# Two experts with split products: the moving parts side by side, 448 + 224 columns in place of 3 x 224

## The chip, the cores and the metric

The kernel runs on one core of a Trainium2 chip, as one program. TensorE (PE) multiplies and transposes, VectorE (DVE) and ScalarE (ACT) work on tiles in SBUF and PSUM, GpSimd (POOL) moves and combines, SyncE (SP) issues most of the DMAs. The metric is the device time of one execution in microseconds (us), the median of several runs.

## The reference

Attention, then a mixture of experts, then a gated MLP over the same 1792 rows:

```python
scores = where(mask, -1e9, q @ k.T / sqrt(64))          # 4 x 12 heads, 448 x 64, causal
x = softmax(scores) @ v                                 # -> (1792, 768)
# experts: the 14336 pairs (token, expert) in descending order of x @ w_gate;
# each token goes to one expert, each of the 8 experts takes 224 tokens
h = np.maximum(x[mask] @ w1[e], 0.0)                    # 224 x 768 @ 768 x 1024
out[mask] = h @ w2[e]                                   # 224 x 1024 @ 1024 x 768
gate = 1.0 / (1.0 + np.exp(-(x @ w_gate)))              # 768 -> 1536
val = x @ w_val
return (gate * val) @ w_out                             # 1536 -> 768
```

Inputs and outputs are fp32 (the weights of the MLP come as 64-bit numbers that the kernel converts).

## The kernel before

**Stages.** Attention until about 285 us; routing and the eight experts until 603.6; the MLP for the first 896 rows (`moe2a`) until about 878; for the other 896 rows (`moe2b`, with seven products of half size in place of eight) until the end. Line 778 (`mm`) issues nearly all matmuls.

**Two kinds of products.** Experts 0 to 5 multiply in fp32. Experts 6 and 7 (`SPLIT`, line 670) and the MLP use split numbers: each operand is a high part, rounded to the matmul's fast 32-bit format, and a low part, the rest. A product then takes three passes: high weight by high token part, high by low, low by high (`prod`, lines 835 to 843; `prods`, line 781, in the MLP).

**An expert.** `xprep` (line 810) transposes the 224 gathered rows into `xx`, 6 blocks of 128 features by 224 tokens; for experts 6 and 7 ACT writes the high part to `xx` (line 823), DVE the low part to `xl` (line 825). `moe` (line 830) runs two layers. Layer 1: 8 outputs of 128 features, each the sum of 6 products; two outputs share one PSUM tile `g` of 512 columns. ACT takes relu and the high part (line 862), DVE the low part (line 864), both 448 wide, into `hx`. Layer 2: 6 outputs, each the sum of 8 products over `hx`. For experts 6 and 7 ACT copies an output to `x2f` (line 895), and after expert 7 the tile is stored to DRAM (line 897) for `moe2b`. The weights of experts 6 and 7 come as `raw`; ACT line 689 writes the high part, DVE line 690 the low part, into two of eight rotating buffers `w`, which PE frees as it goes.

**The start of the MLP.** `conv_split` (lines 79 to 95) makes high and low parts of the MLP weights: lines 83, 85 and 93 on ACT, 87, 88, 89, 92 and 94 on DVE, from a buffer `cs` (two of them) that lines 74 and 77 load; the converted weights are stored to `wsc` by lines 719 (from `ca`), 724 and 725 (high and low part of an output chunk). A gate product goes through a sigmoid on ACT (line 964), is multiplied with the value product on DVE (line 967) and split into `hx` (`h_parts`: ACT line 944, DVE line 945). The tile of the sigmoid lies in memory that the experts' tiles held, `x2f` among them, so the first sigmoid waits for the store of line 897. After two such blocks `out_stage` (line 906) multiplies `hx` with the output weights, in 84 passes of 384 columns.

**What sets the order.** PE's instructions stand in the order of the code. A scheduler places those of the other engines, once, before the program runs; on the chip each engine works through its own list in order, and an instruction that waits holds all behind it. PSUM tiles `g` rotate among 7 buffers.

Of the kernel before, what the change touches and what calls it, by code (L numbers as in the profile page):

```python
# [7 lines left out]
F32 = mybir.dt.float32  # L8
F32R = mybir.dt.float32r
# [3 lines left out]
AF = mybir.ActivationFunctionType  # L13
OP = mybir.AluOpType
# [6 lines left out]
CAP = 224  # L21
E = 8
KD = 6
# [7 lines left out]
def body(ctx: ExitStack, tc: tile.TileContext, q, k, v, moe_w_gate, moe_w1, moe_w2,  # L31
         w_gate2, w_val2, w_out2, out):
    nc = tc.nc
# [171 lines left out]
    ms = att.enter_context(tc.manual_schedule())  # L205
# [261 lines left out]
    mp = ctx.enter_context(tc.tile_pool(name="mp", bufs=2))  # L467
    ps = ctx.enter_context(tc.tile_pool(name="ps", bufs=1, space=PSUM))
# [303 lines left out]
    def use(key):  # L772
        while key not in W:
            load_chunk()
        return W[key]

    def mm(o, a, b, first, last_):
        nc.tensor.matmul(o, a, b, start=first, stop=last_)  # L778
        tick(max(b.shape[-1] * (4.0 if b.dtype == F32 else 1.0) / 2.4, 107.0))
# [9 lines left out]
    XE, X2, X2F = {}, {}, {}  # L789
# [3 lines left out]
    def gathers():  # L793
        while gat["n"] <= gat["x"] and gat["n"] in have:
            with tc.high_priority(HO):
                gather(gat["n"])
            gat["n"] += 1
# [12 lines left out]
    def xprep(ph):  # L810
        xs = XE[ph]
        sp = ph in SPLIT
        xx = mo.tile([128, KD, CAP], F32R if sp else F32, name="xx", bufs=2)
        xl = mo.tile([128, KD, CAP], F32R, name="xl", bufs=1) if sp else None
        for dp in range(3):
            w = ps.tile([128, 512], F32, name="g", bufs=7)[:, :4 * P].rearrange("p (a h q) -> p a h q", a=2, h=2)
            for h in range(2):
                for dd in range(2):
                    d = 2 * dp + dd
                    nc.tensor.transpose(w[:, dd, h, :], xs[h][:, d * 128:(d + 1) * 128], ident[:P, :P])  # L820
            wf = w.rearrange("p a h q -> p a (h q)")
            dd_ = slice(2 * dp, 2 * dp + 2)
            nc.scalar.activation(xx[:, dd_], wf, AF.Copy)
            if sp:
                nc.vector.tensor_tensor(xl[:, dd_], wf, xx[:, dd_].bitcast(F32), op=OP.subtract)
        XE[ph] = (xx, xl) if sp else xx
        gat["x"] = ph + 1
        gathers()

    def moe(ph, nxt):  # L830
        xx = XE[ph]
        hs_ = []
        sp = ph in SPLIT

        def prod(o, w, x, first, last_):

            if sp:
                (wh_, wl_), (xh_, xl_) = w, x
                mm(o, wh_, xh_, first, False)
                mm(o, wh_, xl_, False, False)  # L840
                mm(o, wl_, xh_, False, last_)
            else:
                mm(o, w, x, first, last_)

        def each(t, f):
            return tuple(f(x) for x in t) if sp else f(t)
        for c in range(4):
            w = each(use(("w1", ph, c)), lambda t: t.rearrange("p (c f) -> p c f", c=KD))
            if c % 2 == 0:
                if sp:  # L850
                    h2 = mp.tile([128, 2, 4, CAP], F32R, name="hx", bufs=3)
                    hs_.append((h2[:, 0], h2[:, 1]))
                else:
                    hs_.append(mp.tile([128, 4, CAP], F32, name="hx", bufs=3))
            g = ps.tile([128, 512], F32, name="g", bufs=7)
            for f in range(2):
                for d in range(KD):
                    prod(g[:, f * CAP:(f + 1) * CAP], each(w, lambda t: t[:, d, f * 128:(f + 1) * 128]),
                         each(xx, lambda t: t[:, d]), d == 0, d == KD - 1)
            hx = each(hs_[c // 2], lambda t: t[:, 2 * (c % 2):2 * (c % 2) + 2])  # L860
            gg = g[:, :2 * CAP].rearrange("p (a t) -> p a t", a=2)
            nc.scalar.activation(hx[0] if sp else hx, gg, AF.Relu)
            if sp:
                nc.vector.scalar_tensor_tensor(hx[1], gg, 0.0, hx[0].bitcast(F32), op0=OP.max, op1=OP.subtract)
        blk, half = divmod(ph, 2)
        if half == 0:
            if blk < 2:
                X2[blk] = [[xq() for _ in range(2)] for _ in range(2)]
            else:
                X2F[blk] = mo.tile([128, KD, 448], F32, name="x2f", bufs=2)  # L870
        xo = slice(half * CAP, (half + 1) * CAP)
        ws = [use(("w2", ph, c)) for c in range(2)]
        for dp in range(0, KD, 2):
            ys = [ps.tile([128, 512], F32, name="g", bufs=7) for _ in range(2 if dp == 0 else 1)]
            yo = [ys[0][:, :CAP], ys[1][:, :CAP] if dp == 0 else ys[0][:, CAP:2 * CAP]]
            if dp == 2:
                ws += [use(("w2", ph, c)) for c in range(2, 4)]
            for f0, f1 in ((0, 6), (6, 8)) if dp == 0 else ((0, 8),):
                for n in range(2):
                    d = dp + n  # L880
                    for f in range(f0, f1):
                        a = each(ws[2 * (d // 3) + f // 4], lambda t: t.rearrange("p (c f) -> p c f", c=4)
                                 [:, f % 4, (d % 3) * 128:(d % 3) * 128 + 128])
                        prod(yo[n], a, each(hs_[f // 4], lambda t: t[:, f % 4]), f == 0, f == 7)
                    if nxt is not None and f1 == 8 and d == 4:
                        route_until(nxt)
                        with tc.high_priority(HO):
                            xprep(nxt)
            for n in range(2):
                if blk < 2:  # L890
                    x2h, x2l = (t[(dp + n) // 3][:, (dp + n) % 3, xo] for t in X2[blk])
                    nc.scalar.activation(x2h, yo[n], AF.Copy)
                    nc.vector.tensor_tensor(x2l, yo[n], x2h.bitcast(F32), op=OP.subtract)
                else:
                    nc.scalar.activation(X2F[blk][:, dp + n, xo], yo[n], AF.Copy)
        if blk >= 2 and half:
            nc.sync.dma_start(x2_d[blk - 2], X2F[blk])

    def xq():
        return mp.tile([128, 3, 448], F32R, name="xq", bufs=8)  # L900
# [149 lines left out]
    with tc.tile_pool(name="mo", bufs=2) as mo:  # L1050
        route_until(0)
        for _ in range(3):
            step()
        with tc.high_priority(HO):
            xprep(0)
        for ph in range(E):
            moe(ph, ph + 1 if ph + 1 < E else None)
# [32 lines left out]
```

## Time and profile before

| | |
|---|---|
| median of 3 runs | 1127.73 us (1127.5 to 1129.85) |
| profiled execution | 1128.0 us, span 1126.2 us, mean granted clock 0.981 |
| PE busy | 1077.0 us (96%) |
| DVE busy | 696.0 us (62%) |
| ACT busy | 439.6 us (39%) |
| POOL busy | 276.1 us (25%) |
| chain that ended last | PE 77%, DVE 9%, DMA 8%, other 6% |

A matmul's duration in the trace runs from its start to the modelled end of its results; it overlaps the next one. How fast PE goes is read from start to start. PEld is the load of the weights, which each matmul has. [...]

### The profile page before, as it was taken

To read this page: it belongs to the slowest core of one execution; us is meant where nothing else is said; L and a number is where in the kernel's file an instruction comes from. 1 tells how busy PE (TensorE), PEld (TensorE's weight loads), DVE (VectorE), ACT (ScalarE), POOL (GpSimd) and SP (SyncE) were. 2 spreads that over 40 slices of the span, in tenths; PEclk is the share of its full clock that TensorE was granted. 3 is DMA by queue.
4 is the path that set the end of the run, shared out by engine and by line. 5 is a ranking of instruction groups with operands and counts; after the bars stand their busy time and mean duration, and the time that the engine had idled before them with its cause. 6 is when DMAs were issued, how large, how long until landed. Compare 5 with 4: busy or idle time off the path is not lost.

```text
span 1126.2 us, 19875 instructions
## 1 busy us (share of the span) xinstructions
PE 1077.0 (96%) x7401; PEld 1021.0 (91%) x7401; DVE 696.0 (62%) x1980; ACT 439.6 (39%) x846; POOL 276.1 (25%) x379
## 2 busy tenths in 40 slices
PE   6999999982999999999999999999999999999997
PEld 6999999971899999999999899889999999999997
DVE  5777777766545565451566889787745526445545
ACT  4767777740110110122454664433424343323320
POOL 7333333300000000000000000500034846546522
PEclk9999999995899999999999999999999999999999
DMA  9556565525687657777654785654421521230212
GB/s 167 125 123 169 116 165 124 145 77 103 212 218 177 141 181 173 177 190 209 214 169 162 253 268 208 238 202 151 152 84 53 187 96 45 90 107 29 85 56 98
DMA packets 156991, 167.26 MB, mean 149 GB/s; under 512 B 74576, under 2 KB 140128, under 8 KB 156640
## 3 DMA queue, kind: packets, MB, share of 16 engines
q1 hardware_dynamic: 153472, 154.74, 46.3%
q0 software_dynamic: 2496, 11.04, 5.2%
q8 instruction: 58, 0.95, 0.4%
q10 hardware_dynamic: 928, 0.23, 0.1%
q14 instruction: 37, 0.30, 0.1%
HBM read 122.32 MB, written 32.64 MB: 138 GB/s over the span
## 4 chain that ended last, share of the span: by engine, by line
PE 77%; DVE 9%; DMA 8%; issue 2%; ACT 2%; POOL 2%; POOLq 0%; DVEq 0%; ACTq 0%; SPq 0%
PE g L778 54%; PE o L348 8%; PE w L328 4%; DMA wsc<-ca 3%; PE s L295 2%; PE s L296 2%; DMA xg<-x_d,ids 2%; PE w L257 1%; DVE ca L89 1%; DVE ca L92 1%; DVE ca L88 1%; PE r L503 1%; DMA cs<-in_moe_w_out_dram 1%; DVE acc L934 1%; PE g L820 1%
## 5 line engine op out<-in xcount | busy, mean ns | idle before, releaser
L778 PE MATMUL g<-xq,w 128*128 128x448 f32 x1188 | 281.6, 367 | 0.0
L778 PEld LDWEIGHTS g<-xq,w 128*128 128x128 f32 x1188 | 222.7, 188 | 20.8
L778 PE MATMUL g<-w,hx 128*128 128x384 f32 x1008 | 182.3, 338 | 4.4 <-DVE hx L945 2.3
L778 PEld LDWEIGHTS g<-w,hx 128*128 128x128 f32 x1008 | 176.0, 189 | 9.5 <-DVE hx L945 5.8
L778 PE MATMUL g<-xx,w 128*128 128x224 f32 x768 | 151.5, 339 | 0.0
L778 PE MATMUL g<-hx,w 128*128 128x224 f32 x864 | 150.8, 331 | 0.0
L778 PEld LDWEIGHTS g<-hx,w 128*128 128x128 f32 x864 | 137.6, 191 | 1.7
L778 PEld LDWEIGHTS g<-xx,w 128*128 128x128 f32 x768 | 135.1, 191 | 2.1
L778 PE MATMUL g<-xs,w 128*128 128x448 f32 x432 | 124.7, 365 | 0.0
L742 POOL TENSOR_TENSOR w<-cs,w 128x384 fp32r<-128x384 f32 x84 | 84.2, 1022 | 114.1 <-ACT w L741 113.6
L348 PE MATMUL o<-vt,pt 112*112 112x65 f32 x960 | 106.3, 258 | 0.0
L348 PEld LDWEIGHTS o<-vt,pt 112*112 112x112 f32 x960 | 102.0, 178 | 0.0
L298 DVE CUSTOM_DVE_ANT_0 sm<-s,mask 112x112 f32<-112x112 f32 (+1 forms) x192 | 78.5, 444 | 23.2 <-PE s L296 23.0
L306 ACT ACTIVATE sm<-sm,mn 112x112 f32<-112x112 f32 (+1 forms) x192 | 90.4, 522 | 5.2 <-DVE mn L298 5.1
L934 DVE TENSOR_TENSOR acc<-g,acc 128x384 f32<-128x384 f32 x140 | 74.7, 551 | 28.7 <-PE g L778 28.6
L803 POOL DMA_INDIRECT xg<-x_d,ids x16 | 15.4, 961 | 297.3 <-DVE ids L622 106.7
L778 PEld LDWEIGHTS g<-xs,w 128*128 128x128 f32 x432 | 81.1, 188 | 6.2
L268 POOL CAST st<-hi 64x448 fp32r<-64x448 f32 x96 | 53.3, 556 | 133.7 <-ACT hi L263 115.5
L741 ACT ACTIVATE w<-cs 128x384 fp32r<-128x384 f32 x84 | 40.1, 518 | 95.2 <-PE g L778 59.7
L295 PE MATMUL s<-st,st 128*112 128x112 f32 (+1 forms) x192 | 62.3, 340 | 2.9 <-POOL st L268 2.7
L328 PE MATMUL w<-ident,sm 112*112 112x112 f32 x480 | 63.1, 262 | 0.1
L296 PE MATMUL s<-lo,qz 128*112 128x112 f32 (+1 forms) x192 | 56.7, 310 | 0.0
(214 smaller groups left out, 1448.2 us busy)
## 6 DMA issues: line engine op xcount, KB each, us to landing
w<-in_moe_w_dram SPq DMA_DIRECT2D x96, 384.0 KB, 5.8
raw<-in_moe_w_dram SPq DMA_DIRECT2D x32, 384.0 KB, 4.4
cs<-in_moe_w_gate_dram SPq DMA_DIRECT2D x12, 768.0 KB, 4.3
cs<-in_moe_w_val_dram SPq DMA_DIRECT2D x12, 768.0 KB, 4.7
wsc<-ca SPq DMA_DIRECT2D x24, 384.0 KB, 4.6
cs<-in_moe_w_out_dram SPq DMA_DIRECT2D x12, 768.0 KB, 5.0
wsc<-w SPq DMA_DIRECT2D x12, 768.0 KB, 3.7
cs<-wsc SPq DMA_DIRECT2D x24, 384.0 KB, 3.6
```

The lines of the kernel that those rows point to most:

```text
L268: nc.gpsimd.tensor_copy(st[r, h], hi[r].bitcast(F32))
L295: nc.tensor.matmul(ss[j], qq[:, j, qs], kh[:, j, :w], start=True, stop=False)
L296: nc.tensor.matmul(ss[j], QZ[u % NZ][:, j, qs], kl[:, :w], start=False, stop=True)
L298: nc.vector.tensor_tensor_reduce(sm[:, j, :w], ss[j], mask[:, S - w:], op0=OP.add, op1=OP.min, scale=1.0, scalar=3.0e38, accum_out=mn[:, j ...
L306: nc.scalar.activation(sm[:, j, :w], sm[:, j, :w], AF.Exp, bias=mn[:, j:j + 1], scale=-1.0)
L328: nc.tensor.transpose(w[:P, n, :], sm[:, j, c * P:(c + 1) * P], ident[:P, :P])
L348: nc.tensor.matmul(o[:, n, j, :], pt[:, j * (i + 1) + c, :], vt[:, j, c, :], start=c == 0, stop=c == i)
L741: nc.scalar.activation(hi, src, AF.Copy)
L742: nc.gpsimd.tensor_tensor(lo, src, hi.bitcast(F32), op=OP.subtract)
L778: nc.tensor.matmul(o, a, b, start=first, stop=last_)
L803: g_ = nc.gpsimd.indirect_dma_start(out=xg, out_offset=None, in_=x_d[:], in_offset=bass.IndirectOffsetOnAxis(ap=ids[ph][:, h:h + 1], axis=0))
L934: nc.vector.tensor_tensor(ac, po[:, :384], ac, op=OP.add)
```

## The change

For experts 6 and 7 the high and the low part of the tokens lie side by side: `x2` is 6 blocks of 2 x 224, and `hx` 4 x (2 x 224). A product is one pass of the high weights over all 448 columns and one pass of the low weights over the 224 high columns, into the left half of the same output. So an output has two halves, left (high by high, low by high) and right (high by low), which are summed: ACT copies the right half to a new tile `sd` (two buffers), DVE adds it to the left half. In layer 1 the sum goes back to PSUM, and relu (ACT) and low part (DVE) follow, 224 wide per output; in layer 2 the sum goes to `x2f`. In the last product of an output the two passes stand in the other order. Each output now has a PSUM tile of its own. `xx` of experts 0 to 5 has one buffer in place of two.

```diff
     def xprep(ph):
...
-        xx = mo.tile([128, KD, CAP], F32R if sp else F32, name="xx", bufs=2)
-        xl = mo.tile([128, KD, CAP], F32R, name="xl", bufs=1) if sp else None
+        xx = mo.tile([128, KD, CAP], F32, name="xx", bufs=1) if not sp else None
+        x2 = mo.tile([128, KD, 2, CAP], F32R, name="x2", bufs=1) if sp else None
...
-            nc.scalar.activation(xx[:, dd_], wf, AF.Copy)
             if sp:
-                nc.vector.tensor_tensor(xl[:, dd_], wf, xx[:, dd_].bitcast(F32), op=OP.subtract)
+                nc.scalar.activation(x2[:, dd_, 0], wf, AF.Copy)
+                nc.vector.tensor_tensor(x2[:, dd_, 1], wf, x2[:, dd_, 0].bitcast(F32), op=OP.subtract)
+            else:
+                nc.scalar.activation(xx[:, dd_], wf, AF.Copy)
...
             if sp:
-                (wh_, wl_), (xh_, xl_) = w, x
-                mm(o, wh_, xh_, first, False)
-                mm(o, wh_, xl_, False, False)
-                mm(o, wl_, xh_, False, last_)
+                (wh_, wl_), xf = w, x.rearrange("p b t -> p (b t)")
+                ms = [(o, wh_, xf), (o[:, :CAP], wl_, xf[:, :CAP])]
+                for n_, (o_, a, b) in enumerate(ms[::-1] if last_ else ms):
+                    mm(o_, a, b, first and n_ == 0, last_ and n_ == 1)
...
+                o = g[:, :2 * CAP] if sp else g[:, f * CAP:(f + 1) * CAP]
+                for d in range(KD):
+                    prod(o, each(w, lambda t: t[:, d, f * 128:(f + 1) * 128]), xx[:, d], d == 0, d == KD - 1)
                 if sp:
...
+                    h2 = hx[:, 2 * (c % 2) + f]
+                    tmp = mo.tile([128, CAP], F32, name="sd", bufs=2)
+                    nc.scalar.activation(tmp, o[:, CAP:], AF.Copy)
+                    nc.vector.tensor_tensor(o[:, :CAP], o[:, :CAP], tmp, op=OP.add)
+                    nc.scalar.activation(h2[:, 0], o[:, :CAP], AF.Relu)
+                    nc.vector.scalar_tensor_tensor(h2[:, 1], o[:, :CAP], 0.0, h2[:, 0].bitcast(F32), op0=OP.max,
+                                                   op1=OP.subtract)
...
-            ys = [ps.tile([128, 512], F32, name="g", bufs=7) for _ in range(2 if dp == 0 else 1)]
+            ys = [ps.tile([128, 512], F32, name="g", bufs=7) for _ in range(2 if dp == 0 or sp else 1)]
...
+                elif sp:
+                    tmp = mo.tile([128, CAP], F32, name="sd", bufs=2)
+                    nc.scalar.activation(tmp, yo[n][:, CAP:], AF.Copy)
+                    nc.vector.tensor_tensor(X2F[blk][:, dp + n, xo], yo[n][:, :CAP], tmp, op=OP.add)
```

What the scheduler makes of it, at three places (before expert 6 every engine's list is as it was). Lines behind `moe` carry numbers higher by 14 to 16 in the changed kernel: 980 is the sigmoid (964 before), 960 and 961 are `h_parts` (944, 945), 948 the copy to `acc` (932), 913 the store of `x2f` (897).

First place: PE in expert 7, from the last products of layer 1 (`g_7903`, `g_7864`) to the first of layer 2; `w_7893` and `w_7942`, after the change `w_7836` and `w_7882`, are high parts of weights, `w_7894`, `w_7943`, `w_7837` and `w_7883` low parts. Before:

```order
L778 MATMUL g_7903<-xx_7686,w_7893 128x224
L778 MATMUL g_7903<-xl_7687,w_7893 128x224
L778 MATMUL g_7903<-xx_7686,w_7894 128x224
L778 MATMUL g_7962<-hx_7754,w_7942 128x224 x2
L778 MATMUL g_7962<-hx_7754,w_7943 128x224
```

After:

```order
L778 MATMUL g_7864<-x2_7643,w_7836 128x448
L778 MATMUL g_7864<-x2_7643,w_7837 128x224 x2
L778 MATMUL g_7864<-x2_7643,w_7836 128x448
L778 MATMUL g_7902<-hx_7706,w_7882 128x448
L778 MATMUL g_7902<-hx_7706,w_7883 128x224
```

The two passes with high weights became one of 448 columns; long and short passes alternate, but for the turned last product of an output.

Second place: ACT in expert 7, from the last conversions of w2 (line 689) on; `hx_7853` and `hx_7799` are the second half of the hidden features. Before:

```order
L689 ACTIVATE w_8025<-raw_8027 128x768
L689 ACTIVATE w_8025<-raw_8031 128x768
L862 ACTIVATE hx_7853<-g_7903 128x448
L895 ACTIVATE x2f_7517<-g_7962 128x224
L895 ACTIVATE x2f_7517<-g_7963 128x224
L93 ACTIVATE w_8143<-ca_8150 128x768
L93 ACTIVATE w_8143<-ca_8163 128x768
L895 ACTIVATE x2f_7517<-g_8014 128x224 x2
L93 ACTIVATE w_8258<-ca_8265 128x768
L85 ACTIVATE sq_8276<-cs_8273 128x768
L895 ACTIVATE x2f_7517<-g_8085 128x224 x2
```

After:

```order
L689 ACTIVATE w_7954<-raw_7960 128x768
L866 ACTIVATE sd_7877<-g_7864 128x224
L868 ACTIVATE hx_7799<-g_7846 128x224
L868 ACTIVATE hx_7799<-g_7864 128x224
L908 ACTIVATE sd_7936<-g_7902 128x224
L908 ACTIVATE sd_7939<-g_7903 128x224
L93 ACTIVATE w_8049<-ca_8056 128x768
L93 ACTIVATE w_8049<-ca_8069 128x768
L908 ACTIVATE sd_7996<-g_7942 128x224
L908 ACTIVATE sd_7999<-g_7943 128x224
L908 ACTIVATE sd_8036<-g_8002 128x224
L908 ACTIVATE sd_8039<-g_8003 128x224
```

One relu of 448 became a copy and two relus of 224 behind the same conversions; the last two copies of an output moved ahead of the third line 93 and of line 85. On DVE the matching adds and the subtract stand behind the two conversions of line 690 in the same way, and the four adds of the later outputs among lines 87 to 92.

Third place: SP around the second load of a gate chunk. Before:

```order
L74 DMA cs_8528<-in_moe2_w_val_dram 128x6x256
L724 DMA wsc_63<-w_8373 128x1536
L725 DMA wsc_63<-w_8374 128x1536
L74 DMA cs_8630<-in_moe2_w_gate_dram 128x6x256
L719 DMA wsc_63<-ca_8520 128x768
```

After:

```order
L74 DMA cs_8434<-in_moe2_w_val_dram 128x6x256
L724 DMA wsc_63<-w_8279 128x1536
L74 DMA cs_8536<-in_moe2_w_gate_dram 128x6x256
L725 DMA wsc_63<-w_8280 128x1536
L719 DMA wsc_63<-ca_8426 128x768
```

The load went ahead of the second store; it feeds the line 83 that stands ahead of a copy of `hx` on ACT. That piece of ACT's list, `hx_8286` and `hx_8192` being the second of the two blocks that the first output stage reads. Before:

```order
L83 ACTIVATE cs_8630<-cs_8630 128x768
L93 ACTIVATE w_8513<-ca_8533 128x768
L85 ACTIVATE sq_8633<-cs_8630 128x768
L944 ACTIVATE hx_8286<-g_8308 128x448
L964 ACTIVATE gv_8349<-g_8330 128x448
```

After:

```order
L83 ACTIVATE cs_8536<-cs_8536 128x768
L960 ACTIVATE hx_8192<-g_8214 128x448
L93 ACTIVATE w_8419<-ca_8439 128x768
L85 ACTIVATE sq_8539<-cs_8536 128x768
L980 ACTIVATE gv_8255<-g_8236 128x448
```

The copy of `hx` moved ahead of lines 93 and 85.

## Rows read from the trace of the kernel before

**Rows 1.** Busy table by stage: busy us by engine (instructions), clock, DMA share, GB/s.

```profile
285.00:603.60 318.60, 317.46 (x2456) 308.35 (x2457) 165.81 (x663) 74.39 (x142) 13.04 (x14) 1.00 0.68 183
603.60:878.60 275.00, 270.85 (x1379) 252.37 (x1378) 209.96 (x287) 125.86 (x184) 46.22 (x35) 0.99 0.53 181
```

**Rows 2.** The same table (PE, PEld, DVE, ACT, POOL), 5 us of expert 7.

```profile
575.00:580.00 5.00, 5.00 (x47) 5.00 (x47) 2.36 (x3) 2.45 (x4) 0.00 (x0) 1.00 0.90 292
```

**Rows 3.** Time line of PE: start us, length us, instructions merged, their count.

```profile
554.21 13.56 PE L778 MATMUL g<-hx,w 128*128 128x224 f32 x120
...
571.46 0.27 PE L778 MATMUL g<-xx,w 128*128 128x224 f32 x1
...
603.62 29.36 PE L778 MATMUL g<-xq,w 128*128 128x448 f32 x144
...
651.17 29.92 PE L778 MATMUL g<-xq,w 128*128 128x448 f32 x144
```

**Rows 4.** Time line of matmuls and weight loads (PEld): expert 6; before 632.81.

```profile
553.89 0.19 PEld L778 LDWEIGHTS g<-xl,w 128*128 128x128 f32 x1
553.99 0.27 PE L778 MATMUL g<-xl,w 128*128 128x224 f32 x1
554.00 0.19 PEld L778 LDWEIGHTS g<-xx,w 128*128 128x128 f32 x1
...
632.61 0.56 PEld L778 LDWEIGHTS g<-w,hx 128*128 128x128 f32 x3
```

**Rows 5.** Groups by line and shape: count, busy us, mean ns, idle before.

```profile
L893 DVE TENSOR_TENSOR xq<-g,xq 128x224 fp32r<-128x224 f32 x24 | 9.2, 383 | 5.2 <-ACT xq L892 5.1
...
L895 ACT ACTIVATE x2f<-g 128x224 f32<-128x224 f32 x20 | 6.3, 352 | 18.6 <-PE g L778 18.6
```

**Rows 6.** Time line of DVE and ACT where layer 1 of expert 7 ends.

```profile
588.50 1.83 DVE L690 TENSOR_TENSOR w<-raw,w 128x768 fp32r<-128x768 f32 x2 [1.66 <-ACT w L689]
590.25 0.62 DVE L864 SCALAR_TENSOR_TENSOR hx<-g,hx 128x448 fp32r<-128x448 f32 x1
...
587.62 1.58 ACT L689 ACTIVATE w<-raw 128x768 fp32r<-128x768 f32 x2 [2.01 <-PE g L778]
589.11 0.53 ACT L862 ACTIVATE hx<-g 128x448 fp32r<-128x448 f32 x1
```

**Rows 7.** Chain that ended last, 586 to 640: start us, length us, what.

```profile
594.33 0.85 ACT w L93
...
604.56 9.79 DMA x_d<-x2f
...
623.74 7.96 DMA cs<-in_moe_w_gate_dram
...
631.72 0.90 ACT cs L83
...
635.22 0.51 DVE hx L945
```

**Rows 8.** Time line of PE: first output stage of the MLP, later one.

```profile
632.81 0.69 PE L778 MATMUL g<-w,hx 128*128 128x384 f32 x3
634.64 0.62 PE L778 MATMUL g<-w,hx 128*128 128x384 f32 x2 [1.14 <-ACT hx L944]
635.81 15.53 PE L778 MATMUL g<-w,hx 128*128 128x384 f32 x79 [0.55 <-DVE hx L945]
...
818.04 14.73 PE L778 MATMUL g<-w,hx 128*128 128x384 f32 x84
832.61 27.64 PE L778 MATMUL g<-xq,w 128*128 128x448 f32 x133
```

**Rows 9.** Busy table as in rows 1, single microseconds, clock last but two.

```profile
636.00:637.00 1.00, 1.00 (x4) 1.00 (x4) 1.00 (x2) 0.00 (x0) 0.00 (x0) 0.54 0.00 0
...
638.00:639.00 1.00, 1.00 (x5) 1.00 (x4) 1.00 (x2) 1.00 (x2) 0.00 (x0) 0.50 0.73 209
```

**Rows 10.** Time line of SP's queue: the second store of w.

```profile
622.83 0.34 SPq L725 DMA_DIRECT2D wsc<-w  x1
```

More of the change, by code (lines that the diff above doesn't have):

```diff
@@ L822, in xprep @@
             dd_ = slice(2 * dp, 2 * dp + 2)
-            nc.scalar.activation(xx[:, dd_], wf, AF.Copy)
             if sp:
-                nc.vector.tensor_tensor(xl[:, dd_], wf, xx[:, dd_].bitcast(F32), op=OP.subtract)
-        XE[ph] = (xx, xl) if sp else xx
+                nc.scalar.activation(x2[:, dd_, 0], wf, AF.Copy)
+                nc.vector.tensor_tensor(x2[:, dd_, 1], wf, x2[:, dd_, 0].bitcast(F32), op=OP.subtract)
+            else:
+                nc.scalar.activation(xx[:, dd_], wf, AF.Copy)
+        XE[ph] = x2 if sp else xx
         gat["x"] = ph + 1
@@ L845, in each @@
         def each(t, f):
-            return tuple(f(x) for x in t) if sp else f(t)
+            return tuple(f(x) for x in t) if isinstance(t, tuple) else f(t)
         for c in range(4):
@@ L849, in moe @@
             if c % 2 == 0:
-                if sp:
[L851 to L864, printed above, removed]
+                hs_.append(mp.tile([128, 4, 2, CAP], F32R, name="hx", bufs=3) if sp
+                           else mp.tile([128, 4, CAP], F32, name="hx", bufs=3))
+            hx = hs_[c // 2]
+            gs_ = []
+            for f in range(2):
+                if sp or f == 0:
+                    g = ps.tile([128, 512], F32, name="g", bufs=7)
+                o = g[:, :2 * CAP] if sp else g[:, f * CAP:(f + 1) * CAP]
+                for d in range(KD):
+                    prod(o, each(w, lambda t: t[:, d, f * 128:(f + 1) * 128]), xx[:, d], d == 0, d == KD - 1)
+                if sp:
+                    h2 = hx[:, 2 * (c % 2) + f]
[5 more added lines that the diff above has]
+                                                   op1=OP.subtract)
+            if not sp:
+                nc.scalar.activation(hx[:, 2 * (c % 2):2 * (c % 2) + 2],
+                                     g[:, :2 * CAP].rearrange("p (a t) -> p a t", a=2), AF.Relu)
         blk, half = divmod(ph, 2)
@@ L873, in moe @@
         for dp in range(0, KD, 2):
-            ys = [ps.tile([128, 512], F32, name="g", bufs=7) for _ in range(2 if dp == 0 else 1)]
-            yo = [ys[0][:, :CAP], ys[1][:, :CAP] if dp == 0 else ys[0][:, CAP:2 * CAP]]
+            ys = [ps.tile([128, 512], F32, name="g", bufs=7) for _ in range(2 if dp == 0 or sp else 1)]
+            if sp:
+                yo = [y[:, :2 * CAP] for y in ys]
+            else:
+                yo = [ys[0][:, :CAP], ys[1][:, :CAP] if dp == 0 else ys[0][:, CAP:2 * CAP]]
             if dp == 2:
@@ L883, in moe @@
                                  [:, f % 4, (d % 3) * 128:(d % 3) * 128 + 128])
-                        prod(yo[n], a, each(hs_[f // 4], lambda t: t[:, f % 4]), f == 0, f == 7)
+                        prod(yo[n], a, hs_[f // 4][:, f % 4], f == 0, f == 7)
                     if nxt is not None and f1 == 8 and d == 4:
```

## The prediction

> **What bounds the kernel now.** I read the busy table by stage first. From 285 to 603.6 us (routing and the eight experts) PE is busy 317.5 of 318.6 us, from 603.6 to 878.6 (first half of the gated MLP) 270.9 of 275 [rows 1]. In the two experts that the change touches, DVE and ACT are each busy about 2.4 us of 5 and PE 5.0 of 5 [rows 2]. So PE sets the pace there, and what counts is the distance from the start of one pass to the start of the next, not the mean of a matmul (which overlaps its neighbours).
>
> The time line of PE gives those distances. 120 passes of 224 columns take 13.56 us, the last one's own 0.27 included: 119 starts in 13.29, 111.7 ns each. 144 passes of 448 columns from 603.62 on take 29.36 with 0.37 for the last: 202.7 ns each; 144 from 651.17 on need 206.6 [rows 3]. Twice the columns cost 1.8 times, not twice. The reason shows in the loads: each weight load starts about 10 ns after the matmul before its own, and its own matmul starts about 100 ns later [rows 4]. One load is ahead and no more; before a 448-column pass the load starts 0.20 us ahead, that is again with the pass before [rows 4]. A 224-column pass is therefore as long as the load that runs under it.
>
> Then I followed the chain that ended last through the end of expert 7. It leaves PE at 594.3 and comes back to PE's work only through hx: the conversion of the first MLP weights, the store of x2f (9.8 us from 604.56), the load of a gate weight (8.0 us from 623.74), ACT line 83 at 631.72 and the low part of hx at 635.2 [rows 7]. PE waits for it in the first output stage of the MLP: 84 passes take from 632.81 to 651.17, 18.36 us, where the same 84 later take 14.57 (818.04 to 832.61) [rows 3, 8]. [...]
>
> **The change part by part.** *Passes.* 192 products (2 experts, 2 layers, 48 each) have three passes of 224 now: 576 x 111.7 = 64.3 us. Afterwards each has one of 448 and one of 224. A 448-column pass hides the load of its follower; the 224-column pass that follows has the next load under it and stays at 111.7. Pair: 202.7 + 111.7 = 314.4 ns, 192 of them 60.4 us, so -4.0 us; with 206.6 it is -3.2. No row shows the two lengths in turn. I take -3.6, midway, since both rows are the same shape and neither is nearer.
>
> [...]
>
> *Summing and copying.* Per output the change adds an ACT copy of the right half, a DVE add, and splits the old 448-wide relu and subtract in two. Nearest rows: 224 wide, ACT 352 ns, DVE 383 ns [rows 5]. In the first layer of an expert: ACT 16 x 0.352 less 4 x 0.53 = +3.5 us, DVE 16 x 0.383 less 4 x 0.62 = +3.6 [rows 5, 6]; in the second: DVE 6 x 0.383 = +2.3, ACT nothing (six copies before, six now). About 6 us of DVE and 3.5 of ACT in some 30 us in which each is half idle [rows 2]: hidden by PE as long as PE is never the one that waits.
>
> It waits where layer 1 turns into layer 2. The last two conversions of w2 can start only when PE has freed the buffer, and stand ahead of the last relu on ACT and of the last subtract on DVE, before and after (second place of the order). Now: ACT 587.62, DVE till 590.33, hx whole at 590.87 [rows 6]; layer 2 starts at 571.46 + 144 x 0.1117 = 587.54 and needs it 36 passes, 4.02 us, on, at 591.56. Spare: 0.7 us. Afterwards in expert 7: add behind the two conversions (2.71 after 587.62), then 0.38 + 0.35 + 0.38 and three hand-overs of 0.05: 3.97; needed 13 products x 0.314 = 4.09 after the start of layer 2, which is 4.01 on the same count. Spare: nothing. In expert 6 a subtract stands between the two conversions on DVE, so 0.3 late. I put down +0.35 us for both turns; bounds 0 and +1.5.
>
> *Buffers.* Outputs take 8 and 6 PSUM tiles per expert in place of 4 and 4, out of 7 that rotate; seven outputs ahead is 7 x 1.9 = 13 us of PE, against chains of 2 to 4 us: nothing. One copy of xx in place of two: its readers are done a whole layer before the next is written: nothing. The transposed input goes to the same three copies and subtracts.
>
> *What follows.* So PE enters the MLP 3.25 us earlier, near 600.4. Does the chain behind it come earlier too? The conversions of the first MLP weights wait for w buffers that PE frees (594.3 now) and move with PE by some 2.8 us. On DVE four adds of 0.38 stand among them, 1.5 us if none falls into a gap, so the chain moves by 1.3 to 2.8; I take 2. The store of x2f gains more: now the last two copies stand behind ACT lines 93 and 85, which wait for DVE; in the new order all four copies stand ahead of them. Last product 600.4, copy and add 0.35 + 0.38 and hand-overs: store issued near 601.2 in place of 604.56, landing near 610.6 to 611, and the sigmoid that waits for it 3.5 us earlier.
>
> And one transfer changes its place: the second gate load stood behind both stores of w, the later issued at 622.83, and took 8.0 us [rows 7, 10]; it now goes between them (third place), which takes one of the two out of its way. Shared evenly among the three, 8.0 us is 2.7 each; I take 2. On ACT the hx copy it delays now stands right behind line 83, not behind lines 83, 93 and 85, 1.5 us less. Sum for the first low hx of the pair: 635.7 less 2.0 (chain) less 2 less 1.5 is near 630; PE asks for it at 632.81 + 0.7 - 3.25 = 630.3. The stall of 3.8 us should all but go, clock drop included. Not everything behind it can be placed to 1 us (the half for the other token block is asked for 6.3 us later and hangs on the next load), so I leave 1.0 us in it: -2.8. Bounds: 0 and -3.8.
>
> Sum against the profiled execution of 1128.0 (span 1126.2, 1.8 around it): -3.6 + 0.35 - 2.8 = -6.05, 1121.95. That execution lies 0.27 above the median of the runs, so 1121.7; rounded 1121.8. After that stall PE idles for 4.1 - 1.7 = 2.4 us of the stage [rows 1, 8], so a shift of PE's work reaches the end.
>
> **The rivals.** (1) *The stall stays.* The landing of that gate load depends on everything in the DMA queues, and a wait in line on ACT can be taken up by the next. Then only the passes count: 1127.7 - 3.25 = 1124.5. For: the chain after 604 is DMA for 18 us of 30 [rows 7]. Against: both transfers that it hangs on start earlier.
> (2) *The gain is eaten.* The chain doesn't move at all, since it ends in transfers; PE arrives 3.25 us earlier and waits 3.25 longer: 1127.7. Against: store and loads are started by work that PE releases.
> (3) *Slower.* The turn from layer 1 to layer 2 is late by more than about 1.5 us, because a wait for a raw weight on ACT or DVE holds the copy, and PE loses its clock as it does at 633 to 639. Price of one such stall by that row: 3.8 us; in both experts 7.6, less 3.6: +4.0, 1131.7. It decides from a chain of about 5.5 us against the 4.0 worked out above. Against: ACT and DVE are half idle there.
> (4) *The loads are hidden altogether.* If a second load could run under a 448-column pass, a 224-column pass would cost half a long one, 101 ns: 304 per product, -6.0 us, and with the stall's -2.8 and +0.35: 1119.3. The rows of the loads speak against it: each starts with the pass before its own. [...]
>
> **How the numbers follow.** Forecast (passes, and most of the stall) 0.50, its own range 1120.0 to 1123.5; (1) 0.25, 1123.6 to 1125.8; (2) 0.10; (3) 0.08; (4) 0.07. The range leaves out (2), (3) and part of (4): 1119.6 to 1126.0. A measurement of this kernel tells about 0.2% from no change, 2.3 us, so faster means below 1125.5: forecast, (4) and nine tenths of (1), 0.79; same 0.13; slower 0.08.
>
> **What would show it.** In the changed kernel: 96 passes of 448 and 96 of 224 per expert with 203 to 207 and about 112 ns from start to start; the turns with PE idle under 0.5 us; the first product of the MLP near 600.4; the x2f store issued near 601; the first output stage in 15 to 16 us without a clock under 1. The forecast is wrong if the 224-column pass isn't 112 next to a long one, if PE idles over 1 us in an expert, or if the first output stage still takes over 18 us.

## The result and the profile after

| | before | after |
|---|---|---|
| median (range), five runs each | 1129.68 us (1127.5 to 1131.27) | 1119.71 us (1117.82 to 1122.21) |
| ratio after to before | | 0.9909, 95% 0.9894 to 0.9924 |
| profiled execution | 1128.0, span 1126.2 | 1119.71, span 1118.0 |

The change takes 0.8 to 1.1% off; the forecast was 0.5%. Between these medians lie 9.97 us, where the forecast had 5.9. Of the 8.25 us between the two profiled spans, 0.27 lie ahead of expert 6, 3.17 in the two experts, and 4.81 in the first four output stages of the MLP. Apart from these nothing differs: first MLP product to last matmul, less what the first four output stages take over 14.57 us each, is 508.2 us in both.

The experts first, by the busy table as in [rows 1], before and after; a stretch is one expert, from its first product to the next first product.

```profile
537.98:571.46 33.48, 33.48 (x303) 33.48 (x301) 16.90 (x22) 16.04 (x28) 0.00 (x0) 1.00 0.69 221
571.46:603.62 32.16, 32.16 (x291) 32.16 (x289) 20.08 (x26) 14.46 (x25) 0.00 (x0) 1.00 0.37 116
```

```profile
537.71:570.10 32.39, 31.94 (x206) 30.10 (x205) 21.83 (x39) 19.28 (x41) 0.00 (x0) 1.00 0.70 227
570.10:600.18 30.08, 30.08 (x194) 28.74 (x192) 24.57 (x43) 16.26 (x35) 0.00 (x0) 1.00 0.38 111
```

Expert 7 gained 2.08 us on 96 products, 21.7 ns each: 335.0 before, 313.3 now. Expert 6 gained 1.09, so 0.99 stayed behind in it; PE's row shows where, at the turn to layer 2 (PE's time line):

```profile
556.25 0.90 PE L778 MATMUL g<-hx,w 128*128 128x224 f32 x5
557.53 1.21 PE L778 MATMUL g<-hx,w 128*128 128x224 f32 x4 [0.39 <-ACT hx L868]
```

The two lengths inside a product, from three narrow stretches of the same view (a row begins with the oldest pass still running and bears that pass's shape):

```profile
575.10 0.59 PE L778 MATMUL g<-x,w 128*128 128x448 f32 x3
...
575.32 0.59 PE L778 MATMUL g<-x,w 128*128 128x224 f32 x3
...
575.42 0.48 PE L778 MATMUL g<-x,w 128*128 128x224 f32 x2
```

A long pass starts at 575.10, the short one behind it 0.22 later, the next pass 0.10 after that: 212 and 102 ns by unrounded starts (medians of 137 and 136 passes with a neighbour of the other length on both sides), where the prediction had 202.7 and 111.7 from [rows 3]. Their sum is nearly the one predicted. The starts of the weight loads lie closer to the two old lengths; three in a row, read in the same way:

```profile
575.95 0.19 PEld L778 LDWEIGHTS g<-x,w 128*128 128x128 f32 x1
...
576.05 0.19 PEld L778 LDWEIGHTS g<-x,w 128*128 128x128 f32 x1
...
576.26 0.19 PEld L778 LDWEIGHTS g<-x,w 128*128 128x128 f32 x1
```

From load to load expert 7 takes 108 ns across a short pass and 204.5 across a long one (medians of 64, unrounded), close to the lengths of [rows 3]: a load starts 3 ns behind the start of a short pass and 9.5 behind that of a long one.

Then the start of the MLP: PE, SP's queue, ACT, as in [rows 3, 7, 8, 10].

```profile
600.18 29.35 PE L778 MATMUL g<-xq,w 128*128 128x448 f32 x144
629.36 7.30 PE L778 MATMUL g<-w,hx 128*128 128x384 f32 x41
637.48 7.75 PE L778 MATMUL g<-w,hx 128*128 128x384 f32 x43 [0.82 <-DVE hx L961]
645.07 15.24 PE L778 MATMUL g<-xq,w 128*128 128x448 f32 x73
...
601.19 0.33 SPq L913 DMA_DIRECT2D x_d<-x2f  x1
...
618.43 0.37 SPq L74 DMA_DIRECT2D cs<-in_moe_w_gate_dram  x1
619.25 0.34 SPq L725 DMA_DIRECT2D wsc<-w  x1
...
608.06 1.28 ACT L980 ACT_TABLE_LOAD   x1 [3.06 <-DMA x_d<-x2f]
...
625.23 0.91 ACT L83 ACTIVATE cs<-cs 128x768 uint32<-128x768 uint32 x1 [2.92 <-DMA cs<-in_moe_w_gate_dram]
626.03 0.53 ACT L960 ACTIVATE hx<-g 128x448 fp32r<-128x448 f32 x1
```

The stage takes 645.07 - 629.36 = 15.71 us where it took 18.36 [rows 3, 8]. The x2f store is issued at 601.19 and its wait ends at 608.06. The gate load takes 6.8 us from 618.43 to the start of line 83 (8.0 before, [rows 7]), and the hx copy starts 0.8 behind line 83 in place of 2.3. The clock granted to PE, in the last column but two as in [rows 9], doesn't fall; every microsecond of the stage reads 1.00, this one among them:

```profile
638.00:639.00 1.00, 1.00 (x7) 1.00 (x6) 1.00 (x2) 0.74 (x3) 0.00 (x0) 1.00 0.89 270
```

The later stages hold what the prediction missed. The table gives, for every run of this study, what the first four output stages took over 14.57 us, start to start (PE's time line; the other stages differ by at most 0.3):

```
                  1st   2nd   3rd   4th    sum   MLP lists of
before            3.79  0.00  3.35  0.80   7.94  before
stage9_before     2.56  2.58  0.00  4.28   9.42  before, GpSimd's work later
short6            2.39  2.73  4.52  0.10   9.74  before, PE 2.1 us earlier
hp_before         1.98  2.52  4.62  1.11  10.23  before, as they were
swap_before       2.09  2.50  5.20  0.40  10.19  before, one piece of after
hxfirst_before    1.78  2.86  4.79  0.60  10.03  before, one piece of after
hold_before       1.55  2.06  2.07  0.00   5.68  before, one piece of after
orders_before     2.42  1.46  2.10  0.00   5.98  before, all three pieces
after             1.14  1.16  0.83  0.00   3.13  after
after_again       1.63  0.68  0.00  0.00   2.31  after
long6             0.57  1.79  0.00  0.00   2.36  after, PE 2.4 us later
unswap_after      0.42  1.57  0.00  0.00   1.99  after, one piece undone
hp_after          0.53  0.52  0.20  0.00   1.25  after, as they were
nosum             6.56  0.48  1.26  0.20   8.50  of its own
```

So the profile of before that the prediction read (3.79, then none) was not typical: `short6` and `hp_before`, which have its lists from the MLP on, stall in the second stage as well and lose 9.74 and 10.23 us in all, and with one piece moved it is 9.4 to 10.2 (but for `hold_before`, below). Experts 3.1 us and stages some 7 us make the 10 us between the medians; the 7 is what is left of the 10, and the rows above leave room for 6 to 9.

A part of the 3.79 has a reason of its own. The clock fell, and PE did less: its rows of a microsecond count 4 and 5 passes at 0.54 and 0.50 [rows 9], and 7 at 1.00 in the same place (after, above; `hp_before`, below). A clock of 0.50 stands in this stage of this profile alone: in the other seven runs of the old order each microsecond of the first stage reads 1.00, as here in `hp_before`.

```profile
638.00:639.00 1.00, 1.00 (x7) 1.00 (x6) 1.00 (x3) 0.02 (x1) 0.00 (x0) 1.00 0.20 49
```

### The profile page after: what moved, and what is told of

Read it like the earlier page. It is cut to its first block, busy times and chain, and to the rows that moved or that the text cites. A ratio compares the mean times of both kernels' runs of the same rounds, so it can differ in the third digit from the quotient of the medians.

```text
span 1118.0 us, 19588 instructions
## 1 busy us (share of the span) xinstructions
PE 1071.0 (96%) x7209; PEld 1013.0 (91%) x7209; DVE 705.4 (63%) x2016; ACT 445.4 (40%) x870; POOL 274.8 (25%) x379
## 4 chain that ended last, share of the span: by engine, by line
PE 80%; DVE 9%; DMA 6%; issue 2%; POOL 2%; ACT 1%; POOLq 0%; SPq 0%; DVEq 0%; ACTq 0%
PE g L778 57%; PE o L348 8%; PE w L328 4%; PE s L295 2%; DMA wsc<-ca 2%; PE s L296 2%; DMA cs<-in_moe_w_gate_dram 2%; PE r L503 2%; PE w L257 1%; DVE ca L88 1%; DVE ca L89 1%; DVE ca L92 1%; DVE w L94 1%; PE g L821 1%; DMA xg<-x_d,ids 1%
## 5 line engine op out<-in xcount | busy, mean ns | idle before, releaser
L778 PE MATMUL g<-w,hx 128*128 128x384 f32 x1008 | 179.4, 335 | 2.4 <-DVE hx L961 2.2
L778 PE MATMUL g<-hx,w 128*128 128x224 f32 (+1 forms) x768 | 149.5, 349 | 0.4 <-ACT hx L868 0.4
L778 PEld LDWEIGHTS g<-hx,w 128*128 128x128 f32 x768 | 134.2, 190 | 4.5 <-issue 0.8
L778 PE MATMUL g<-xx,w 128*128 128x224 f32 x576 | 120.0, 363 | 0.0
L778 PEld LDWEIGHTS g<-xx,w 128*128 128x128 f32 x576 | 106.5, 192 | 2.5 <-issue 0.4
```

## The experiments

### Is it PE's place in time, or the order of the other engines' lists?

`short6`: before, expert 6 with 30 passes left out.

```diff
-                mm(o, wh_, xl_, False, False)
+                dropped.append(0) if ph == E - 2 and not first and not last_ and len(dropped) < 30 else mm(o, wh_, xl_, False, False)
```

> The kernel before, but 30 of the high-by-low passes of expert 6 are left out (its output lacks those terms). ACT, DVE, POOL and SP have the lists of the kernel before from expert 7 on; only PE reaches the MLP 30 x 111.7 ns = 3.35 us earlier, as it does after the change. Theory 'order' (what the change gained in the output stages comes from the new order of loads, conversions and hx copies): the four first output stages stay at 18.4, 14.6, 17.9 and 15.4 us, time -3.35 us against before, ratio 0.997. Theory 'shift' (it comes from PE's work lying 3.3 us earlier against everything else): the stages become 15.7, 15.7, 15.4 and 14.6 us as in the changed kernel, time -8.1 us, ratio 0.993. Third possibility, the stalls hang on transfers that PE does not release: they grow by 3.35 us, ratio 1.000.

`long6`: after, 30 passes of expert 6 twice.

```diff
-                    mm(o_, a, b, first and n_ == 0, last_ and n_ == 1)
+                    [mm(o_, a, b, first and n_ == 0, last_ and n_ == 1) for _ in range(2 if ph == E - 2 and not (first or last_ or n_ == 0) and (added.append(0) or len(added) <= 30) else 1)]
```

> The changed kernel, with 30 passes of 224 columns in expert 6 done twice (its output is then wrong by those terms). The other engines keep the lists of the changed kernel from expert 7 on; PE reaches the MLP 30 x 0.104 to 0.112 = 3.1 to 3.4 us later, where it was before the change. Theory 'order': the first four output stages stay at 15.7, 15.7, 15.4 and 14.6 us, time 3.2 us over the changed kernel, ratio to before 0.9955. Theory 'shift': the stalls of before return (18.4, 14.6, 17.9, 15.4 us), time 8 us over the changed kernel, ratio 1.000.

Measured: `short6` 0.9989 of before (0.9970 to 1.0008), `long6` 0.9933 (0.9911 to 0.9954), and the changed kernel in the next set (`after_again`) 0.9912 (0.9892 to 0.9932). From the start of expert 6 to the MLP `short6` takes 63.56 us in place of 65.64: only 2.1 less of the 3.35 left out, since expert 6 now loses 1.3 more at its turn of layers. `long6` takes 64.86 in place of 62.47, 2.4 more, since the turn's stall is gone. In both the stalls stay with the lists: `short6` has 9.74 us of them, `long6` 2.36, with PE at 630.8 and 633.3 at the first stage against 632.8 and 629.4. From the first MLP product to the end of the span `short6` takes 524.4 us, among the 522.6 to 525.4 of the old order (without `hold_before` and `orders_before`), and `long6` 517.0, among the 515.9 to 517.8 of the new; so in the profiles PE's shift reaches the end. The time of `short6` (1.2 us less, interval 3.4 less to 0.9 more) can't tell 2.1 from nothing, but it leaves no room for the 8 of "shift". The third stage of `long6`, then of `short6` (PE's time line):

```profile
724.33 14.73 PE L778 MATMUL g<-w,hx 128*128 128x384 f32 x84
```

```profile
724.54 0.69 PE L778 MATMUL g<-w,hx 128*128 128x384 f32 x3
726.70 0.62 PE L778 MATMUL g<-w,hx 128*128 128x384 f32 x2 [1.47 <-ACT hx L944]
727.92 15.87 PE L778 MATMUL g<-w,hx 128*128 128x384 f32 x79 [0.60 <-DVE hx L945]
```

They start this stage 0.2 us apart; one runs through, the other loses 4.5. "Shift" falls: the order decides.

### What stalls the third stage

In before it looks so: PE, then ACT (time lines), then DVE's groups from 717 to 724 (count, busy us, mean ns).

```profile
725.25 0.69 PE L778 MATMUL g<-w,hx 128*128 128x384 f32 x3
726.21 0.62 PE L778 MATMUL g<-w,hx 128*128 128x384 f32 x2 [0.27 <-ACT hx L944]
...
735.60 7.72 PE L778 MATMUL g<-w,hx 128*128 128x384 f32 x43 [1.17 <-DVE hx L945]
743.17 2.02 PE L778 MATMUL g<-xq,w 128*128 128x448 f32 x9
...
712.75 0.91 ACT L83 ACTIVATE cs<-cs 128x768 uint32<-128x768 uint32 x1 [3.06 <-DMA cs<-in_moe_w_out_dram]
713.56 1.57 ACT L93 ACTIVATE w<-ca 128x768 fp32r<-128x768 f32 x2
...
725.61 0.54 ACT L944 ACTIVATE hx<-g 128x448 fp32r<-128x448 f32 x1 [9.62 <-DVE g L967]
```

```profile
L88 DVE SCALAR_TENSOR_TENSOR ca<-cs,ca 128x768 uint32<-128x768 uint32 x2 | 3.7, 1912 | 0.0
L89 DVE CUSTOM_DVE_ANT_0 ca<-cs,ca 128x1536 uint16<-128x1536 uint16 x2 | 3.7, 1902 | 0.0
```

The copy of hx waits 9.62 us for the multiply (line 967), which stands on DVE behind lines 88 and 89; these take twice their usual 0.95 us. GpSimd's subtractions for the second half (lines 989 to 991) run beside them, from 717.16 on.

`stage9_before`: the same work of GpSimd two chunks later.

```diff
-            if f == NF // 2 + 1:
+            if f == NF // 2 + 3:
```

> The kernel before with the call of stage() (GpSimd's subtractions for the second half, lines 989 to 991, and four loads on SP) two chunks later; the lists of all other engines are as before. Theory 'GpSimd slows DVE': lines 88 and 89 take 0.95 us in place of 1.9 where GpSimd no longer works beside them (717 to 724 us), the third output stage falls from 17.9 us to under 15.5, and the time by 2.4 us or less (ratio 0.998 to 1.000, since GpSimd's work now lies beside a later stage and may stall that). Rival, DVE's list alone makes the stall: the third stage stays at 17.9 us, ratio 1.000.

PE's time line, and DVE's groups from 717 to 724, then from 763 to 771, where GpSimd now works:

```profile
725.74 14.73 PE L778 MATMUL g<-w,hx 128*128 128x384 f32 x84
...
771.94 0.61 PE L778 MATMUL g<-w,hx 128*128 128x384 f32 x2 [1.20 <-ACT hx L944]
...
781.32 7.75 PE L778 MATMUL g<-w,hx 128*128 128x384 f32 x43 [1.19 <-DVE hx L945]
```

```profile
L88 DVE SCALAR_TENSOR_TENSOR ca<-cs,ca 128x768 uint32<-128x768 uint32 x2 | 1.8, 952 | 0.0
...
L88 DVE SCALAR_TENSOR_TENSOR ca<-cs,ca 128x768 uint32<-128x768 uint32 x2 | 3.7, 1905 | 0.0
```

The stall left the third stage and stands in the fourth (0 and 4.28 us); the time is that of before, 1.0005 (0.9990 to 1.0021). DVE's list is that of before, so GpSimd's part in it is shown.

`hold_before`: why has the changed kernel next to none of it, with the same work of GpSimd in the same chunk? ACT's lists differ here. In before, line 83 for the second output half, which waits for its load until 712.75 above, stands ahead of two lines 93; in after behind them. This run moves it in before.

```diff
-        nc.scalar.activation(lw, lw, AF.Copy, scale=2.0 ** -29)
+        a83 = lambda: nc.scalar.activation(lw, lw, AF.Copy, scale=2.0 ** -29); in_order(tc, a83, l93[-1][1]) if nx in (('wo', 6, 1),) else a83()
```

> The kernel before with one piece of the change's order on ACT: line 83 for the second output half of f = 6, which waits for its load, goes behind the two lines 93 of the gate chunk and no longer ahead of them, as in the changed kernel. Up to there all lists are as before. Theory: in the order of before that waiting line holds lines 93, 94 and so the conversions of DVE back until GpSimd's subtractions run beside them, and the multiply behind them is late; in the new order the third output stage falls from 3.4 to 5.2 us over 14.57 to under 1, the first two stay at 3.8 to 5.1 in all, time -3.5 us, ratio 0.997. Rival (DVE's own list, or GpSimd whatever stands ahead): the third stage keeps over 3 us, ratio 1.000.

ACT, then PE:

```profile
710.76 1.57 ACT L93 ACTIVATE w<-ca 128x768 fp32r<-128x768 f32 x2
714.36 0.91 ACT L83 ACTIVATE cs<-cs 128x768 uint32<-128x768 uint32 x1 [2.03 <-DMA cs<-in_moe_w_out_dram]
...
725.50 7.67 PE L778 MATMUL g<-w,hx 128*128 128x384 f32 x41
734.56 7.74 PE L778 MATMUL g<-w,hx 128*128 128x384 f32 x43 [1.39 <-DVE hx L945]
```

0.9965 of before (0.9952 to 0.9979), 4.0 us (2.4 to 5.4). Lines 93 start 14.7 us ahead of the stage in place of 11.7, and DVE is through both lines 88 before GpSimd starts at 718.8. The waits for the first half of hx are gone, that for the second stays: 2.07 us, not under 1 as expected. The edit names one line, but the scheduler moved more behind it: on DVE a line 92 now stands ahead of the multiply, as in after, and in the next chunk line 83 goes behind lines 93 too, which it doesn't in after (the fourth stage then has no stall). So some 4 of the 7 us hang on one line on ACT that waits for a load and on what the scheduler made of moving it; the third stage alone, at 3.35 to 5.20 in the old order, accounts for 1.3 to 3.1 of them.

### The pieces that the prediction named, in the first stage

`swap_before` puts the gate load between the two stores of w, in the first two chunks.

```diff
-            nc.sync.dma_start(o_[:, 1], lo.bitcast(F32))
+            held.append((o_, lo)) if c in (0, 2) else nc.sync.dma_start(o_[:, 1], lo.bitcast(F32))
...
-            conv_load(kind, f, n, cs)
+            ld = conv_load(kind, f, n, cs)
+        if held and f % 2: o, l = held.pop(); late(ld, o, l)
```

> The kernel before with one piece of the change's order alone: in the first two chunks the second gate load goes between the two stores of w on SP, as in the changed kernel. On ACT and DVE only two lines move (line 83 and one low part of hx, each by one or two places). If this swap is what shrank the first output stage, as the prediction has it: the first two stages together go from 3.8 to 5.1 us over their undisturbed length (before, stage9_before, short6) to about 2.3 (changed kernel), the third keeps its 3.4 to 4.5 us; time -2 us, ratio 0.998. Rival, what counts is where the multiply and the parts of hx stand among the conversions on DVE and ACT, and the swap does nothing: first two stages stay at 3.8 to 5.1 us, ratio 1.000.

`unswap_after` undoes that in the changed kernel.

```diff
-        with tc.issue_after(xst[-1]):
+        with tc.issue_after((lost if lost and kind == "gv" and f % 2 and n == 0 else xst)[-1]):
```

> The changed kernel with that piece undone: the second gate load goes behind both stores of w on SP in the first two chunks; one line 83 on ACT and one line 94 on DVE move by a place. If the swap is what shrank the first output stage: the first two stages go from 2.3 us over their undisturbed length back to 3.8 or more, time +2 us over the changed kernel, ratio 0.993. Rival (the place of the hx parts counts): they stay at 2.3 us, ratio 0.991.

`hxfirst_before` puts the hx copy directly behind line 83 on ACT.

```diff
-        nc.scalar.activation(sq, hw.bitcast(F32), AF.Square)
+        a85 = lambda: nc.scalar.activation(sq, hw.bitcast(F32), AF.Square); in_order(tc, a85, hxa[{('gv', 3, 0): (1, 0)}[nx]]) if nx in {('gv', 3, 0): (1, 0)} else a85()
...
-        nc.scalar.activation(hn, w_, AF.Copy)
+        a93 = lambda: nc.scalar.activation(hn, w_, AF.Copy); in_order(tc, a93, hxa[{('gv', 2, 1): (1, 0)}[nx]]) if nx in {('gv', 2, 1): (1, 0)} else a93()
```

> The kernel before with another piece: in the first output stage the copy of hx (line 944) stands directly behind line 83 on ACT, ahead of lines 93 and 85, as in the changed kernel; nothing else on ACT moves, on DVE line 94 goes behind the low part of hx. If the place on ACT counts: the copy starts 0.8 us behind the start of line 83 in place of 2.3, the first stage falls from 2.0 to 3.8 us over 14.57 to 0.5 to 2, time -1.5 us, ratio 0.999. Rival (the load of the gate chunk sets it): first stage as before, ratio 1.000.

Ratios: `swap_before` 0.9987 (0.9973 to 1.0001), `unswap_after` 0.9920 (0.9900 to 0.9940), `hxfirst_before` 0.9993 (0.9978 to 1.0009). None can be told from the kernel it was made from. Each did its own work: with the swap line 83 starts 6.2 us after the load's issue (623.08 to 629.27), against 6.9 to 8.5 in the six runs of the old order that keep both stores ahead; with the copy in front it starts 0.8 behind line 83. And the stage can't be told from the old order's all the same (2.09 and 1.78 us over 14.57, against 1.55 to 2.56 without the clock's fall); the 1.78 lies in the 0.5 to 2 that was expected, the time doesn't show it. `short6` (old order), then `hxfirst_before`, PE's time line of the first stage:

```profile
632.24 0.61 PE L778 MATMUL g<-w,hx 128*128 128x384 f32 x2 [0.77 <-ACT hx L944]
633.42 6.54 PE L778 MATMUL g<-w,hx 128*128 128x384 f32 x36 [0.56 <-DVE hx L945]
640.16 7.73 PE L778 MATMUL g<-w,hx 128*128 128x384 f32 x43 [0.20 <-DVE hx L945]
```

```profile
631.00 7.41 PE L778 MATMUL g<-w,hx 128*128 128x384 f32 x41
639.76 7.75 PE L778 MATMUL g<-w,hx 128*128 128x384 f32 x43 [1.35 <-DVE hx L945]
```

The waits for the first token block are gone, 1.33 us by these rows, and the wait for the second has grown from 0.20 to 1.35: PE only gets to it sooner. In this run it is the next hx, one gate load further, that sets the stage.

`orders_before`: the three pieces together.

> The kernel before with the three pieces at once (gate load between the stores, hx copy behind line 83, line 83 of the output half behind lines 93); PE's work is that of before. If these three are what the change gained behind the experts: first stage under 1.6 us, third under 1, second 2.5 as before, in all about 4 in place of 7.9 to 10.2; time -5 us, ratio 0.995. If the gain needs the expert passes or something else in the lists: over 7 us left, ratio 0.998 to 1.000.

0.9969 (0.9955 to 0.9982), stalls 5.98 us where about 4 was expected: what `hold_before` has alone. The first two pieces add nothing that can be seen.

### Other ways to order hx, and the changed kernel again

`hp_before` and `hp_after` give the gate multiply and the parts of hx priority with the scheduler.

```diff
-                nc.vector.tensor_tensor(pv[:, :448], pv[:, :448], gv, op=OP.mult)
-                h_parts(hx, bb, pv[:, :448])
+                with tc.high_priority(HO):
+                    nc.vector.tensor_tensor(pv[:, :448], pv[:, :448], gv, op=OP.mult); h_parts(hx, bb, pv[:, :448])
```

> The kernel before, with the gate multiply and the two parts of hx given high priority, so that on DVE they stand ahead of the conversions; ACT, SP, POOL and PE keep their lists. If the stalls of the output stages (7.9 to 9.7 us in all) are hx standing behind conversions on DVE: they fall to the 1.3 us that the same edit leaves in the changed kernel, time -6 to -8 us, ratio 0.993 to 0.995. Rival (loads and ACT's list hold hx back): they stay above 5 us, ratio 0.998 to 1.000.

> The changed kernel with the gate multiply and the two hx parts of the first half given high priority, so that on DVE they stand ahead of the weight conversions. If what is left of stalls in the output stages (1.1, 1.2, 0.8 us over 14.57) is DVE's list alone: all stages near 14.6 us, 3 us under the changed kernel, ratio to before 0.988. Rival, the conversions fall behind and PE waits for converted weights (w) instead: same time as the changed kernel or up to 4 us slower, ratio 0.991 to 0.995.

`hp_before` 0.9999 (0.9987 to 1.0012), stalls 10.2 us: in its third stage the multiply still stands behind both pairs of lines 88 and 89 on DVE and starts at 728.71, 1 us after the stage. `hp_after` 0.9915 (0.9897 to 0.9933), stalls 1.25 us. The priority moved nothing: in the traces DVE (491 instructions in before, 493 in after), ACT, SP and GpSimd work from the first MLP product to the end in the order of before and of after, one for one. So neither expectation was put to a test, and whether hx standing behind conversions on DVE makes these stalls is untested. What the two runs are is one more profile of each order.

`after_again`: no edit.

> The changed kernel once more, beside the others on one chip. Time ratio 0.991; a second profile tells how far the stalls of one profile can be trusted: the four output stages at 1.1, 1.2, 0.8 and 0 us over 14.57 if they belong to the order, another split with the same sum (about 3 us) if they vary from run to run.

0.9912, stalls 2.3 us in the first four stages and 0.29 in the fifth. The split varies from run to run, the sum less: the four profiles with the changed kernel's lists in the MLP (`after`, `after_again`, `long6`, `hp_after`) have 1.25 to 3.13 us.

### What the sums cost

`nosum`: no copy of the right half, no add, in both layers.

```diff
-                    nc.scalar.activation(tmp, o[:, CAP:], AF.Copy)
-                    nc.vector.tensor_tensor(o[:, :CAP], o[:, :CAP], tmp, op=OP.add)
```

> The changed kernel without the sums: the right half (high weights by low tokens) is multiplied but neither copied nor added, so the output lacks it; no tile sd, no adds. Tells what copies and adds cost in the experts: if they are hidden but for the turn of expert 6, experts 6 and 7 take 62.5 us with them (65.6 before the change) and 61.6 to 61.7 without; if PE pays for each output, 28 x 0.05 us or more come off. The lists in the MLP change too, so the whole time says little: ratio 0.988 to 0.994.

Experts 6 and 7 take 61.50 us (538.20 to 599.70) where the changed kernel takes 62.47: the sums cost 0.97, all of it at the turn of expert 6. Yet the time is 0.9915 (0.9891 to 0.9938), no better. The scheduler wrote other lists, and in the first stage the copies of an output to `acc`, which free PSUM, now stand on ACT behind a line 83 that waits 2.60 us for its load and a line 93 that waits 1.69 us for DVE. PE's time line, and the busy table of a microsecond behind the waits:

```profile
628.89 6.43 PE L778 MATMUL g<-w,hx 128*128 128x384 f32 x36
637.26 1.43 PE L778 MATMUL g<-w,hx 128*128 128x384 f32 x5 [1.94 <-ACT acc L948]
639.77 10.41 PE L778 MATMUL g<-w,hx 128*128 128x384 f32 x43 [1.08 <-DVE hx L961]
```

```profile
642.00:643.00 1.00, 1.00 (x5) 1.00 (x4) 1.00 (x2) 1.00 (x3) 0.00 (x0) 0.50 0.15 58
```

3.0 us of waits, and the clock at 0.50 for some 6 us (639 to 645), 6.56 us in all. The profiled execution is the slowest of this run's four (1124.62 us, median 1122.43), so it is one draw; still, with 0.97 us less work the time is no shorter.

## Why the prediction was right and wrong

*Passes* (-3.6): right in kind, small by 0.56. 192 x 21.7 ns are -4.16, a little beyond the bound of -4.0. 314.4 ns for a pair was nearly the right sum (313.3) of two wrong lengths; to lean half way to 206.6 cost 0.4 of the 0.56. The prediction would be wrong "if the 224-column pass isn't 112 next to a long one": it is 102, and only because the long pass is longer by as much does the sum hold. That a short pass is as long as the load under it is true of the loads' own pace (108 ns), not of the pass. (The load at 632.61 in [rows 4] stands before a pass of 384 columns, under one of 448, not before one of 448.) Rival (4) had the short pass right (101) but not the long one, which is 212.

*Turn* (+0.35): +0.99, inside the bounds and all in expert 6, where 0.3 was put down; expert 7 loses nothing, as worked out. The 0.05 for a hand-over was the author's estimate, with no row behind it; in the new trace the subtract of expert 6 starts at 557.51, 0.03 behind the end of the relu that it waits for (557.12 + 0.36). Together the experts gave 3.17 of 3.25.

*What follows* is the step that failed. PE reached the MLP where it should (600.18 for 600.4), the store was issued where it should (601.19 for 601.2) and landed at least 2.5 us sooner than thought (608.06 for 610.6 to 611), the load and the copy moved as read from the order. The first stage then kept 1.14 us for the 1.0 set down. But the runs take the reason away: each of the two moves alone, and both together, leave 1.8 to 2.4 us, as the old order does (1.6 to 2.6 but for the one profile with 3.79). The wait moved to the second block, which the prediction saw and put no more than its 1.0 on. And 1.4 to 1.8 of the 3.8 that it wanted to win back (3.79 less the 2.39 and 1.98 of `short6` and `hp_before`, with the same lists) came with the fall of the clock, which no other profile of the old order repeats. The size was right by the luck of that profile.

And the term ended there: "After that stall PE idles for 2.4 us of the stage, so a shift of PE's work reaches the end" treats all later stalls as fixed. The sentence on the shift holds in the profiles (`short6`, `long6`). What fails is to let a stall belong to the place and not to the order: the scheduler had rewritten the lists of ACT and DVE up to about the third stage, not just at the places shown, and stages two to four fell from 4.15 us to 1.99 between the two profiles, by more between typical ones. Recorded idle time also hid the size: 2.4 us of it stood for 4.15 from start to start, with the clock at 1.00 throughout these two stages. The term of -2.8 should have been one for all stalls behind the experts; it measured -4.8 between the profiles and about -7 between the medians.

*Rivals.* The stall shrank (1), though part of that was the clock's fall, and the gain wasn't eaten (2): with the order fixed, an earlier PE doesn't find longer stalls (`short6`, by its profile). No turn cost 1.5 us or the clock (3); that a wait of this length costs the clock isn't shown: it fell behind waits of 1.14 and 0.55 us in before [rows 8, 9], and not behind 0.77, 0.56 and 0.20 in the first stage of `short6`.

*Still open*: `hold_before` explains 4 of about 7 us, with what the scheduler moved behind its line. The first stage (0.4 to 1.6 us in the new order), the second stage (1.5 to 2.9 us in the old order, but for the one profile with none; 0.5 to 1.8 in the new) and the rest of the third were not taken apart; hx behind conversions on DVE was not tested; and why passes of two lengths in turn start at 212 and 102 ns, while their loads start at 204.5 and 108.

## What to carry to other kernels

Where a scheduler orders the other engines, a change on PE is two changes: price the work, and then compare every list down to the end of the phase, above all instructions that wait for a load and stand ahead of work that doesn't need it; one such line, with what hung on it, was worth about as much as the passes (4.0 us, 2.4 to 5.4, against 4.16). Don't count a stall that is removed until the next wait of the same kind is placed, since PE may merely reach that one sooner (0.20 us became 1.35 in `hxfirst_before`). Take the stalls of one profile as one draw: the same lists put 0 to 2.7 us into the second stage. And look in the trace whether an edit to the order moved anything at all, before its time is read as an answer.

## What the chip showed beyond that

GpSimd's subtractions slow some of DVE's lines and not others. Lines 88 and 89 of DVE, whose two inputs lie in SBUF, took 1912 and 1902 ns beside GpSimd's subtractions and 952 and 954 in the same stretch without them (`stage9_before`); line 945, which reads one input from PSUM, took 611 ns wholly beside them and 617 without (the mean of five in before, 650 to 716). GpSimd's and DVE's rows in before:

```profile
726.00 1.86 POOL L990 TENSOR_TENSOR xs<-xs 128x448 f32<-128x448 f32 x1
...
726.78 0.61 DVE L945 TENSOR_TENSOR hx<-g,hx 128x448 fp32r<-128x448 f32 x1
```

What sets the two apart no run took apart: the lines differ in operation and width too.
